# A decode kernel's result: kept as columns and stored from 128 partitions, instead of folded into 16 rows

## The chip, the cores and the metric

The kernel runs on one core of a Trainium2 chip. A core has five engines with queues of their own: TensorE (PE, matmuls; its weight loads are shown as PEld), VectorE (DVE), ScalarE (ACT), GpSimd (POOL) and SyncE (SP, which here only issues transfers). All of them work on SBUF, a memory of 128 partitions; matmuls write to PSUM. Sixteen DMA engines carry the transfers between SBUF and the device's memory (HBM). The metric is device microseconds of one execution. Before the change the median of three runs is 192.62 us (192.46 to 193.06).

## The reference

One token of 512 values goes through attention over a sliding window and through a small MLP that gates it:

```
xn = layernorm(x)                                  # x: [1, 1, 512]
q  = xn @ wq                                       # 32 heads of 128
p  = softmax(q . k[last 4096 positions] * 128**-0.5)
s  = concat_heads(p . v) @ wo                      # [512]
x1 = xn + shifted(gelu(layernorm(xn) @ w1)) @ w2   # all shifts fill with 0 for one token
g  = silu(x1 + gelu(layernorm(x1) @ w3) @ w4)      # [512]
out = x + s * g                                    # [1, 1, 512], bf16
```

With one token every shifted part is zero, so that `x1` is `xn`. The keys and values of 32 heads and 4,096 positions are 33.5 MB each in bf16, and nearly all of the 79 MB that the kernel reads.

## The kernel before

The work goes over the heads in eight groups of four. For each group SyncE issues one load of K (4 MB, three buffers) and, two steps later, one of V (two buffers); the loads stand in program order in SyncE's queue, each behind the wait for its buffer. The scores of a group are computed on two paths: VectorE multiplies a part of the keys with the query and sums (`k_vector`, L334 to L340), and for the rest PE transposes the keys (L356), ScalarE copies them (L359) and PE multiplies (L367). A softmax (`sm_*`) and the product with V (`v_wide`, L440) follow one and two steps later. The order on PE, VectorE and ScalarE is written out by hand in a loop over the steps (L575 to L694); what stands before that loop is ordered by a scheduler.

The front (L101 to L321) loads `x` as 16 rows of 32 values (`x_in`, L80). A matmul and a masked sum bring it to `x_f` (L180), a tile of 128 partitions by 4, where partition p holds the four neighbouring values 4p to 4p+3. From that come the normalised `xn_f` (L183), the query, and the gate. The gate's last products lie in `hr`, a row of 512, and are turned into columns by matmuls (L284). For the gate a second layout is used: column j of `h2_ps` and `g_col` holds the values 128j + p. So `x` is brought into this layout once more (`r_slot`, `r_row`, `r_in`, `xt_ps`, `xn_col`, L239 to L250).

The output product `s` is made in two parts. Heads 0 to 27 are multiplied with `wo` row by row (`y_wide`), summed in `y_sum` (one tile of 512 columns) and transposed into columns (`y_turn`, L553). The last four heads come with the last pieces of V: these are multiplied as columns (`v_part`, L474, into `oP`), `v_turn` (L452) transposes the part that was made wide before, `v_out` (L480) adds both (`both`) and scales them (`o`), and `y_head` (L547) multiplies each head's column with 128 columns of `wo_rows` at a time: 16 matmuls with one moving column, into `y_cols`.

Columns with values 128j + p would be stored as single values. So the kernel multiplies the columns by `g_own` (the gate, spread over four slots with zeros elsewhere) and folds them with a matmul by 0/1 columns (`fold_f`, `fold_bf`) into 16 rows of 32 neighbouring values, `z_rows` (`z_add`, L565). This is done for the first part in fp32 inside the loop (L561, L689), and for the last four heads after it (L696 to L698). VectorE then adds `x_in` (L700), and 16 rows of 64 bytes are stored (L701). `y_cols` and `z_rows` are parts of one PSUM tile, cleared at the start by a matmul with zeros (L305).

Of the kernel before, what the change touches and what calls it, by code (L numbers as in the profile page):

```python
# [8 lines left out]
P = 128  # L9
BF16 = mybir.dt.bfloat16  # L10
FP32 = mybir.dt.float32
# [15 lines left out]
def kernel(  # L27
# [14 lines left out]
    nc = tc.nc  # L42
# [28 lines left out]
    small.tile([P, 240], BF16, name="pad")  # L71
    wts_guard = tc.tile_pool(name="wts", bufs=1)
    wts = wts_guard.__enter__()

# [154 lines left out]
    for j in range(KC):  # L229
        for c in range(KC):  # L230
# [8 lines left out]
    r_slot = wts.tile([XR, KC], BF16, name="r_slot")  # L239
    nc.vector.tensor_reduce(out=r_slot[:], in_=ident_bf[0:XR, 0:XR].rearrange("k (j a) -> k a j", a=KC), axis=AX.X, op=ALU.max)  # L240
    r_row = wts.tile([XR, KC], BF16, name="r_row")
    nc.vector.tensor_reduce(out=r_row[:], in_=ident_bf[0:XR, 0:XR].rearrange("k (j a) -> k j a", a=KC), axis=AX.X, op=ALU.max)
    r_in = wts.tile([XR, KC, XC], BF16, name="r_in")
    nc.vector.tensor_tensor(out=r_in[:], in0=x_in[:].unsqueeze(1).to_broadcast([XR, KC, XC]),
                            in1=r_slot[:].unsqueeze(2).to_broadcast([XR, KC, XC]), op=ALU.mult)
    xt_ps = ps_misc.tile([P, KC], FP32, tag="misc", name="xt_ps")
    nc.tensor.matmul(xt_ps[:], lhsT=r_in[:].rearrange("k a n -> k (a n)"), rhs=r_row[:], start=True, stop=True)
    xn_col = small.tile([P, KC], FP32, name="xn_col")
    nc.vector.tensor_scalar(out=xn_col[:], in0=xt_ps[:], scalar1=negmean[:], scalar2=rstd[:],
                            op0=ALU.add, op1=ALU.mult)  # L250

    a_ps = ps_misc.tile([P, 3, P], FP32, tag="misc", name="a_ps")
    zeros(a_ps[:])
    for c in range(KC):
# [35 lines left out]
    make_masks(16)  # L290
    make_masks(8)
    make_masks(4)
    NQ = P // XC
    g_own = small.tile([P, KC, NQ], FP32, name="g_own")
    nc.gpsimd.tensor_tensor(out=g_own[:], in0=g_col[:].unsqueeze(2).to_broadcast([P, KC, NQ]),
                            in1=masks[4][2][:].unsqueeze(1).to_broadcast([P, KC, NQ]), op=ALU.mult)
    fold_f = const.tile([P, XC], FP32, name="fold_f")
    nc.vector.tensor_reduce(out=fold_f[:], in_=ident_f[:].rearrange("d (i t) -> d t i", t=XC), axis=AX.X, op=ALU.max)
    fold_bf = const.tile([P, XC], BF16, name="fold_bf")
    nc.vector.tensor_copy(out=fold_bf[:], in_=fold_f[:])  # L300
# [127 lines left out]
    def wo_row(h):  # L428
        return wo_rows[:, h - h_part, :]
# [90 lines left out]
                                    op=ALU.add)  # L520
        ox_blk[i] = ox

    small.tile([P, 64], BF16, name="pad_rows")
    y_sum = small.tile([P, D], FP32, name="y_sum")
    small.tile([P, 32], BF16, name="pad_result")

    yr = {}

# [17 lines left out]

    def y_head(h):  # L547
        for j in range(KC):
            nc.tensor.matmul(y_cols[:, j:j + 1], lhsT=wo_row(h)[:, j * P:(j + 1) * P],
                             rhs=o_blk[3][:, h - h_part:h - h_part + 1], start=False, stop=(h == H - 1),  # L550
                             skip_group_check=True)

    def y_turn():  # L553
        yt_ps = ps_misc.tile([P, KC, P], FP32, tag="misc", name="yt_ps")
        for j in range(KC):
            nc.tensor.transpose(yt_ps[:, j, :], y_sum[:, j * P:(j + 1) * P], ident_f[:])
        y_first = small.tile([P, KC], FP32, name="y_first")
        nc.vector.tensor_reduce(out=y_first[:], in_=yt_ps[:].rearrange("p j (i m) -> p j i m", m=32)[:, :, :, 0],
                                axis=AX.X, op=ALU.add)
        t_first = small.tile([P, KC, NQ], FP32, name="t_first")  # L560
        nc.vector.tensor_tensor(out=t_first[:], in0=y_first[:].unsqueeze(2).to_broadcast([P, KC, NQ]), in1=g_own[:],  # L561
                                op=ALU.mult)
        return t_first

    def z_add(t, fold, last):  # L565
        nc.tensor.matmul(z_rows, lhsT=t[:].rearrange("p j q -> p (j q)"), rhs=fold[:], start=False, stop=last,
                         skip_group_check=True)

    NG = H // G
# [5 lines left out]
    for s in range(NG + LAG):  # L575
# [22 lines left out]
        if s < NG:  # L598
            nb = len(batches(s))

            def keys(b0, b1):
                for b in range(b0, b1):
                    k_turn(s, kn, b)
                    if b > 0:
                        k_scores(s, b - 1)

            k_open(s)
            k_vector(s, kn, 0)
            keys(0, 2)
            if s == 7:  # L610
                v_turn(h - 1)
                v_add(h - 1)
                v_out(h - 1)
            elif s > 1:
                sm_den(s - 2)
                sm_rden(s - 2)
            elif s == 1:
                sm_max(0)
            k_vector(s, kn, 1)
            keys(2, 4)  # L620
            if s == 7:
                sm_den(h)
                sm_rden(h)
                keys(4, nb - 2)
                sm_turn(s - 1)
                keys(nb - 2, nb)
            else:
                if s > 0:
                    sm_turn(s - 1)
                keys(4, nb)  # L630
            k_scores(s, nb - 1)
            sm_own(s)
            if s == 7:
                k_vector(s, kn, 2)
                v_wide(h, v)
                sm_exp(s - 1)
                v_turn(h)
                y_open()
                k_vector(s, kn, 3)
                v_add(h)  # L640
                v_out(h)
                ox_spread(1)
                sm_max(s)
                continue
            if s > 0:
# [12 lines left out]
            if s == 6:  # L658
                ox_pick(0)
            if s > 0:  # L660
                sm_max(s)
        elif s == NG:
            ox_pick(1)
            sm_turn(NG - 1)
            sm_exp(NG - 1)
            y_wide(1, False)
            sm_den(NG - 2)
            sm_rden(NG - 2)
            y_wide(0, False)
            warm(3)  # L670
            v_wide(h, v)
            sm_den(NG - 1)
            sm_rden(NG - 1)
            v_turn(h)
            v_add(h)
            v_out(h)
            ox_spread(2)
        else:
            v_open(h)
            warm(2)  # L680
            v_wide(h, v, cuts[1], last=False)
# [4 lines left out]
            t_first = y_turn()  # L686
# [10 lines left out]
    nc.vector.tensor_tensor(out=t_last[:], in0=y_cols.unsqueeze(2).to_broadcast([P, KC, NQ]), in1=g_own[:], op=ALU.mult)  # L697
    z_add(t_last, fold_bf, True)  # L698
    out_sb = small.tile([XR, XC], BF16, name="out_sb")
    nc.vector.tensor_tensor(out=out_sb[:], in0=z_rows, in1=x_in[:], op=ALU.add)  # L700
    load(out.rearrange("a b (r n) -> (a b r) n", r=XR), out_sb[:])  # L701


# [28 lines left out]
```

## Time and profile before

| | |
|---|---|
| profiled execution | 192.31 us |
| its span in the profile | 190.4 us |
| PE busy, clock granted on the mean | 121.9 us (64%), 0.695 |
| VectorE busy | 154.3 us (81%) |
| ScalarE busy | 89.8 us (47%) |
| read from HBM | 78.84 MB, 414 GB/s over the span |
| store of the result, issue to landing | 1.3 us, 1.0 KB |
| first landing of small rows (`x_in`), issue to landing | 2.9 us, 1.0 KB |

The profile is of one execution; 1.91 us of its time lie outside the span. Busy time is time in which an engine runs at least one instruction; neighbouring instructions may overlap. A line of the timeline has start, length, engine, line of the kernel, operation, the tile written and those read, their sizes and a count, and in brackets how long the engine had idled and who ended that. In the chain in order of time each line is a piece that nothing else could have replaced, with its start, its length and what it was. "Issue" in that chain is time without a visible cause.

### The profile page before, as it was taken

The page shows a single profiled execution, that of the slowest core. Times are in us where ns is not written, and L with a number is a line of the kernel's source. Part 1 is how long each engine was busy: PE and PEld are TensorE (multiplying, and loading weights), DVE is VectorE, ACT ScalarE, POOL GpSimd, SP SyncE. Part 2 cuts the span into 40 slices and gives each one's busy share as a digit, 9 for nine tenths or more (in the row PEclk, how much of TensorE's full clock was granted, in tenths as well). Part 3 has the DMA queues.
Part 4 walks back from the last instruction along what each step waited for, and adds up shares of the span by engine and source line. Part 5 has one row for each costly group of instructions (what it writes and reads, how often), then busy time and mean ns, then how long its engine had stood idle before and what let it go on. Part 6 is the DMA issues. An engine that isn't in the chain of part 4 may idle for free.

```text
span 190.4 us, 2822 instructions
## 1 busy us (share of the span) xinstructions
PE 121.9 (64%) x1143; PEld 78.4 (41%) x1143; DVE 154.3 (81%) x184; ACT 89.8 (47%) x192; POOL 2.4 (1%) x11
## 2 busy tenths in 40 slices
PE   2445973977656268436955674572888379748983
PEld 1321442755545243334434333440764068523332
DVE  4830159999999999999999999999999998991111
ACT  2000781778695076517382746452485146754120
POOL 2110000000000000000000000000000000000000
PEclk9999696555555556955596579558555755885999
DMA  6999999999999999999999999999999999999991
GB/s 214 458 404 420 435 427 435 434 441 440 437 442 434 440 434 430 427 434 399 430 427 440 434 437 416 465 434 437 406 434 435 434 420 406 444 434 416 418 389 59
DMA packets 4621, 79.02 MB, mean 415 GB/s; under 512 B 544, under 2 KB 1152, under 8 KB 1664
## 3 DMA queue, kind: packets, MB, share of 16 engines
q1 hardware_dynamic: 4432, 74.65, 91.9%
q10 hardware_dynamic: 176, 4.20, 5.1%
q8 instruction: 9, 0.15, 0.3%
q14 instruction: 4, 0.03, 0.0%
HBM read 78.84 MB, written 0.00 MB: 414 GB/s over the span
## 4 chain that ended last, share of the span: by engine, by line
DVE 56%; DMA 32%; PE 7%; ACT 1%; issue 1%; SPq 1%; DVEq 0%; ACTq 0%
DVE S L340 34%; DMA kv<-in_A_k_cache_dram 24%; DVE prod L338 19%; DMA kv<-in_A_v_cache_dram 8%; PE pt L356 3%; PE ov L444 1%; ACT kt L359 1%; SPq L76 1%; PE sT L367 1%; PE ot_ps L461 1%; DVE m L383 1%; DVE S L381 1%; DVE mx L391 1%; PE oP L477 1%; DVE md L393 0%
## 5 line engine op out<-in xcount | busy, mean ns | idle before, releaser
L340 DVE TENSOR_REDUCE S<-prod 128x20 f32<-128x2560 bf16 (+2 forms) x32 | 87.6, 2736 | 1.1
L359 ACT COPY kt<-pt 128x1024 bf16<-128x1024 bf16 (+1 forms) x51 | 50.0, 1004 | 43.8 <-PE pt L356 42.2
L356 PE MATMUL pt<-ident_f,kv 128*128 128x128 f32 x202 | 48.0, 392 | 11.7 <-DMA kv<-in_A_k_cache_dram 11.7
L338 DVE TENSOR_TENSOR prod<-kv,q_bc 128x2560 bf16<-128x2560 bf16 (+2 forms) x32 | 46.1, 1442 | 2.4 <-DMA kv<-in_A_k_cache_dram 2.1
L356 PEld LDWEIGHTS pt<-ident_f,kv 128*128 128x128 f32 x202 | 35.2, 205 | 15.1 <-DMA kv<-in_A_k_cache_dram 12.3
L367 PE MATMUL sT<-q_pair,kt 128*128 128x8 bf16 x404 | 19.2, 171 | 14.1 <-ACT kt L359 13.9
L367 PEld LDWEIGHTS <-kt 128*128 128x128 bf16 x404 | 16.6, 106 | 25.0 <-ACT kt L359 23.8
L444 PE MATMUL ov<-kv,pT 128*16 128x512 bf16 x248 | 22.7, 528 | 0.7 <-DMA kv<-in_A_v_cache_dram 0.7
L389 PE MATMUL mt_ps<-ident_f,m 128*1 128x128 f32 x8 | 3.0, 372 | 18.3 <-DVE rden L416 17.0
L405 ACT ACTIVATE pT<-S,mb 128x128 bf16<-128x128 f32 x32 | 14.0, 574 | 0.2
L450 ACT COPY ov_sb<-ov 128x512 f32<-128x512 f32 x8 | 4.7, 586 | 18.4 <-PE ov L444 18.4
L444 PEld LDWEIGHTS <-pT 128*16 128x16 bf16 x248 | 6.8, 111 | 13.3 <-issue 11.5
L376 ACT ACTIVATE own<-sT,par 128x48 f32<-128x48 f32 (+2 forms) x32 | 7.5, 352 | 3.7 <-PE sT L367 3.7
L461 PE MATMUL ot_ps<-ident_f,ov_sb 128*128 128x128 f32 x32 | 7.5, 377 | 1.9 <-ACT mb L401 1.6
L208 ACT CAST q_row<-qr_ps 128x512 bf16<-128x512 f32 x1 | 0.6, 586 | 16.8 <-PE qr_ps L206 16.8
L389 PEld LDWEIGHTS mt_ps<-ident_f,m 128*1 128x1 f32 x8 | 0.6, 80 | 18.8 <-DVE rden L416 17.4
L405 ACT ACTIVATION_READ_ACCUMULATOR pT<-S,mb 128x1 f32 x32 | 8.3, 259 | 0.0
L209 DVE CAST q_row<-qr_ps 128x512 bf16<-128x512 f32 x1 | 0.7, 690 | 8.7 <-PE qr_ps L206 8.7
L398 PE MATMUL mb_ps<-md,par_t 5*128 5x4 f32 x16 | 4.3, 335 | 5.0 <-DVE md L393 4.9
L416 DVE RECIPROCAL rden<-den_ps 128x4 f32<-128x4 f32 x8 | 1.4, 175 | 7.2 <-PE den_ps L411 7.2
L398 PEld LDWEIGHTS mb_ps<-md,par_t 5*128 5x128 f32 x16 | 3.8, 291 | 6.0 <-PE sT L367 4.7
L461 PEld LDWEIGHTS ot_ps<-ident_f,ov_sb 128*128 128x128 f32 x32 | 4.8, 188 | 2.5 <-ACT mb L401 2.0
(143 smaller groups left out, 89.8 us busy)
## 6 DMA issues: line engine op xcount, KB each, us to landing
kv<-in_A_k_cache_dram SPq DMA_DIRECT2D x7, 4096.0 KB, 32.2
kv<-in_A_v_cache_dram SPq DMA_DIRECT2D x7, 4096.0 KB, 30.3
wq_sb<-in_A_wq_dram ACTq DMA_DIRECT2D x1, 4096.0 KB, 17.6
kv<-in_A_k_cache_dram SPq DMA_DIRECT2D x2, 2048.0 KB, 25.8
wo<-in_A_wo_dram SPq DMA_DIRECT2D x1, 2048.0 KB, 29.3
kv<-in_A_v_cache_dram SPq DMA_DIRECT2D x1, 2048.0 KB, 13.7
w_sb<-in_B_w_dram SPq DMA_DIRECT2D x1, 1376.0 KB, 12.6
w_sb<-in_B_w_dram SPq DMA_DIRECT2D x1, 1280.0 KB, 18.9
```

Of the source, the lines that this page charges most:

```text
L338: nc.vector.tensor_tensor(out=prod[:, 0:m, :], in0=kn[:, rows, :], in1=q_bc[:, g:g + 1, :].to_broadcast([P, m, Dh]), op=ALU.mult)
L340: nc.vector.tensor_reduce(out=st[g]["S"][:, rows], in_=prod[:, 0:m, :], axis=AX.X, op=ALU.add)
L356: nc.tensor.transpose(pt[:, i, :], kn[:, c:c + 2, :].rearrange("p c d -> p (c d)").bitcast(FP32), ident_f[:])
L359: nc.scalar.copy(out=kts[b][:, 0:n, :], in_=pt[:, 0:n, :].bitcast(BF16))
L367: nc.tensor.matmul(st[g]["sT"][:, c:c + 2, :].rearrange("p c a -> p (c a)"), lhsT=kt[:, i, l::2], rhs=q_pair[:, g, l, :], start=(l == 0), ...
L376: nc.scalar.mul(s["own"][:, 0:m, a], s["sT"][:, 0:m, a], par[:, a:a + 1])
L389: nc.tensor.transpose(mt_ps[:], s["m1"][:], ident_f[:])
L398: nc.tensor.matmul(mb_ps[:], lhsT=par_t[:].rearrange("k b a -> k (b a)"), rhs=md[:], start=True, stop=True)
L405: nc.scalar.activation(out=s["pT"][:, :, a], in_=s["S"][:], func=ACT.Exp, scale=scale, bias=mb[:, a:a + 1], accum_out=s["sum"][:, a:a + 1])
L444: nc.tensor.matmul(ov[r:r + 4 * G], lhsT=s["pT"][:, c:c + 4, :].rearrange("p i a -> p (i a)"), rhs=v[:, c:c + 4, :], start=(i < 4), stop=( ...
L450: nc.scalar.copy(out=s["ov_sb"][:], in_=ov[:])
L461: nc.tensor.transpose(ot_ps[:, step * j:step * j + P], s["ov_sb"][:, j, :], ident_f[:])
```

## The change

The second layout is given up. All that belongs to the output is kept in the layout of `x_f`: partition p, column j holds the value 4p + j. To that end the three products that turn rows into columns take every fourth column of the row (`j::KC`) and not 128 neighbouring ones: `hr` for the gate, `y_sum` in `y_turn`, and `wo_row(h)` in `y_head`. With that `xn_f` itself serves for the gate, and `r_slot`, `r_row`, `r_in`, `xt_ps` and `xn_col` go. `g_own`, `fold_f`, `fold_bf`, `t_first`, `t_last` and both fold matmuls go too. The first part of the product opens the sum in `y_cols` by a matmul with the identity (`y_begin`), which stands after the last pieces of V. After the loop four VectorE operations, one for each column, compute column times gate plus `x`, and the result is stored from 128 partitions with 4 values (8 bytes) each. Three padding tiles grow (`pad`, `pad_rows` and `pad_result`).

```diff
-    r_slot = ... r_row = ... r_in = ...
-    xt_ps = ps_misc.tile([P, KC], FP32, tag="misc", name="xt_ps")
-    nc.tensor.matmul(xt_ps[:], lhsT=r_in[:].rearrange("k a n -> k (a n)"), rhs=r_row[:], start=True, stop=True)
-    xn_col = small.tile([P, KC], FP32, name="xn_col")
-    nc.vector.tensor_scalar(out=xn_col[:], in0=xt_ps[:], scalar1=negmean[:], scalar2=rstd[:],
-                            op0=ALU.add, op1=ALU.mult)
...
-    nc.tensor.matmul(h2_ps[:], lhsT=ident_f[:], rhs=xn_col[:], start=True, stop=False, skip_group_check=True)
+    nc.tensor.matmul(h2_ps[:], lhsT=ident_f[:], rhs=xn_f[:], start=True, stop=False, skip_group_check=True)
     for j in range(KC):
-        nc.tensor.matmul(h2_ps[:, j:j + 1], lhsT=hr[:, j * P:(j + 1) * P], rhs=ind[:], start=False, stop=True,
+        nc.tensor.matmul(h2_ps[:, j:j + 1], lhsT=hr[:, j::KC], rhs=ind[:], start=False, stop=True,
                          skip_group_check=True)
...
-    g_own = ... fold_f = ... fold_bf = ...
-    yz_ps = ps_y.tile([P, KC + XC], FP32, name="yz_ps")
-    nc.tensor.matmul(yz_ps[:], lhsT=zero_bf[:], rhs=zero_bf[:, 0:KC + XC], start=True, stop=False,
-                     skip_group_check=True)
-    y_cols, z_rows = yz_ps[:, 0:KC], yz_ps[0:XR, KC:KC + XC]
+    y_cols = ps_y.tile([P, KC], FP32, name="y_cols")
...
     def y_head(h):
         for j in range(KC):
-            nc.tensor.matmul(y_cols[:, j:j + 1], lhsT=wo_row(h)[:, j * P:(j + 1) * P],
+            nc.tensor.matmul(y_cols[:, j:j + 1], lhsT=wo_row(h)[:, j::KC],
...
     def y_turn():
...
-            nc.tensor.transpose(yt_ps[:, j, :], y_sum[:, j * P:(j + 1) * P], ident_f[:])
+            nc.tensor.transpose(yt_ps[:, j, :], y_sum[:, j::KC], ident_f[:])
...
-        nc.vector.tensor_tensor(out=t_first[:], in0=y_first[:].unsqueeze(2).to_broadcast([P, KC, NQ]), in1=g_own[:],
-                                op=ALU.mult)
-        return t_first
-
-    def z_add(t, fold, last):
-        nc.tensor.matmul(z_rows, lhsT=t[:].rearrange("p j q -> p (j q)"), rhs=fold[:], start=False, stop=last,
+        return y_first
+
+    def y_begin(y_first):
+        nc.tensor.matmul(y_cols[:], lhsT=ident_f[:], rhs=y_first[:], start=True, stop=False,
                          skip_group_check=True)
...
-            z_add(t_first, fold_f, False)
             v_add(h)
             v_part(h, v, cuts[3], CP)
+            y_begin(y_first)
             v_out(h)
...
-    t_last = small.tile([P, KC, NQ], BF16, name="t_last")
-    nc.vector.tensor_tensor(out=t_last[:], in0=y_cols.unsqueeze(2).to_broadcast([P, KC, NQ]), in1=g_own[:], op=ALU.mult)
-    z_add(t_last, fold_bf, True)
-    out_sb = small.tile([XR, XC], BF16, name="out_sb")
-    nc.vector.tensor_tensor(out=out_sb[:], in0=z_rows, in1=x_in[:], op=ALU.add)
-    load(out.rearrange("a b (r n) -> (a b r) n", r=XR), out_sb[:])
+    out_sb = small.tile([P, KC], BF16, name="out_sb")
+    for j in range(KC):
+        nc.vector.scalar_tensor_tensor(out=out_sb[:, j:j + 1], in0=y_cols[:, j:j + 1], scalar=g_col[:, j:j + 1],
+                                       in1=x_f[:, j:j + 1], op0=ALU.mult, op1=ALU.add)
+    load(out.rearrange("a b (p j) -> p (a b j)", p=P), out_sb[:])
```

The scheduler orders the front anew: all 20 matmuls of L259 stand ahead of the 32 of L206 (four stood behind them), and ScalarE takes the Gelu of L262 ahead of the copy of L208, with one load of an activation table fewer. SyncE's transfers and their waits stand in the same order as before.

More of the change, by code (lines that the diff above doesn't have):

```diff
@@ L70 @@
     sm_pool = ctx.enter_context(tc.tile_pool(name="sm", bufs=3))
-    small.tile([P, 240], BF16, name="pad")
+    small.tile([P, 336], BF16, name="pad")
     wts_guard = tc.tile_pool(name="wts", bufs=1)
@@ L237 @@
     nc.vector.tensor_scalar(out=z3_bf[:], in0=xc3[:], scalar1=rstd3[:], scalar2=None, op0=ALU.mult)
[L239 to L245, printed above, removed]
-    xt_ps = ps_misc.tile([P, KC], FP32, tag="misc", name="xt_ps")
-    nc.tensor.matmul(xt_ps[:], lhsT=r_in[:].rearrange("k a n -> k (a n)"), rhs=r_row[:], start=True, stop=True)
-    xn_col = small.tile([P, KC], FP32, name="xn_col")
-    nc.vector.tensor_scalar(out=xn_col[:], in0=xt_ps[:], scalar1=negmean[:], scalar2=rstd[:],
-                            op0=ALU.add, op1=ALU.mult)
     a_ps = ps_misc.tile([P, 3, P], FP32, tag="misc", name="a_ps")
@@ L292 @@
     make_masks(4)
[L293 to L300, printed above, removed]
-    yz_ps = ps_y.tile([P, KC + XC], FP32, name="yz_ps")
-    nc.tensor.matmul(yz_ps[:], lhsT=zero_bf[:], rhs=zero_bf[:, 0:KC + XC], start=True, stop=False,
-                     skip_group_check=True)
-    y_cols, z_rows = yz_ps[:, 0:KC], yz_ps[0:XR, KC:KC + XC]
+    y_cols = ps_y.tile([P, KC], FP32, name="y_cols")
     par = const.tile([P, G], FP32, name="par")
@@ L521, in ox_pick @@
         ox_blk[i] = ox
-    small.tile([P, 64], BF16, name="pad_rows")
+    small.tile([P, 112], BF16, name="pad_rows")
     y_sum = small.tile([P, D], FP32, name="y_sum")
-    small.tile([P, 32], BF16, name="pad_result")
+    small.tile([P, 96], BF16, name="pad_result")
     yr = {}
@@ L559, in y_turn @@
                                 axis=AX.X, op=ALU.add)
-        t_first = small.tile([P, KC, NQ], FP32, name="t_first")
-        nc.vector.tensor_tensor(out=t_first[:], in0=y_first[:].unsqueeze(2).to_broadcast([P, KC, NQ]), in1=g_own[:],
-                                op=ALU.mult)
-        return t_first
-    def z_add(t, fold, last):
-        nc.tensor.matmul(z_rows, lhsT=t[:].rearrange("p j q -> p (j q)"), rhs=fold[:], start=False, stop=last,
+        return y_first
+    def y_begin(y_first):
+        nc.tensor.matmul(y_cols[:], lhsT=ident_f[:], rhs=y_first[:], start=True, stop=False,
                          skip_group_check=True)
@@ L685 @@
             v_wide(h, v, cuts[2], cuts[1])
-            t_first = y_turn()
+            y_first = y_turn()
             v_part(h, v, cuts[2], cuts[3])
             v_turn(h)
-            z_add(t_first, fold_f, False)
             v_add(h)
             v_part(h, v, cuts[3], CP)
+            y_begin(y_first)
             v_out(h)
```

## The prediction

> **What bounds the kernel now.** I read the page's header and the 40 slices first, to see which engine or queue has no room; then the chain of work that ended last; then the chain in order of time and the timeline of the last microseconds; then the DMA issues.
>
> ```profile
> span 190.4 us, 2822 instructions
> PE 121.9 (64%) x1143; PEld 78.4 (41%) x1143; DVE 154.3 (81%) x184; ACT 89.8 (47%) x192; POOL 2.4 (1%) x11
> ...
> DMA  6999999999999999999999999999999999999991
> ...
> DVE 56%; DMA 32%; PE 7%; ACT 1%; issue 1%; SPq 1%; DVEq 0%; ACTq 0%
> ```
>
> Although VectorE (DVE) has 56% of the chain, the DMA row is at 9 in every slice but the first and the last: the loads never pause, so VectorE and the loads keep pace with each other, and an engine that gets ahead in the middle finds no earlier data. What is left to gain or lose lies before the stream starts and after it ends. The end in order of time:
>
> ```profile
> 184.77 0.56 PE oP L477 x16
> 185.32 0.49 PE ot_ps L461 x4
> 185.82 0.16 PE yz_ps L566 x2
> 185.98 0.01 issue
> 185.99 0.57 PE oP L477 x16
> 186.56 0.02 issue
> 186.58 0.17 DVE both L489
> 186.75 0.02 issue
> 186.78 0.17 DVE o L492
> 186.95 0.04 issue
> 186.99 0.60 PE yz_ps L549 x16
> 187.60 0.02 issue
> 187.62 0.19 DVE t_last L697
> 187.81 0.04 issue
> 187.85 0.20 PE yz_ps L566
> 188.05 0.02 issue
> 188.07 0.18 DVE out_sb L700
> ```
>
> The groups at 184.77 and 185.99 begin 0.04 us after a piece of V lands (184.72 and 185.94 in the record of landings), and the 16 matmuls of L549 begin when both `o` and the first piece of `wo_rows` are there (landed 186.95); the second piece lands at 187.29. So up to 187.3 the stream paces the end, with compute a few hundredths behind, and from 187.6 a serial tail runs alone: VectorE, PE, VectorE, the store.
>
> ```profile
> 7.20 0.66 PE L231 MATMUL hs_ps<-shifted_bf,w_sb 128*128 128x1 bf16 x16 [0.25 <-DVE ln_vtot_x L162]
> ...
> 7.25 0.14 DVE L164 TENSOR_SCALAR ln_rstd_x<-ln_vtot_x 128x1 f32<-128x1 f32 x1
> 7.32 0.28 DVE L129 TENSOR_REDUCE blk<-ident_bf 128x32 bf16<-128x128 bf16 x1
> ...
> 8.07 0.23 DVE L184 TENSOR_SCALAR xn_f<-ln_xc_x,ln_rstd_x 128x4 f32<-128x4 f32 x1 [0.29 <-POOL ln_rstd_x L166]
> 8.21 0.19 DVE L132 COPY to<-blk 128x128 bf16<-128x128 bf16 x1
> ...
> 186.99 0.59 PE L549 MATMUL yz_ps<-o,wo_rows 128*128 128x1 bf16 x16 [0.45 <-DVE o L492]
> ...
> 188.28 0.35 SPq L76 DMA_DIRECT2D out_dram<-out_sb  x1
> ```
>
> These rows of the timeline price the new forms: a weight read that skips by four (L231) beside a dense one (L549), a small VectorE operation with a per-partition scalar (L184) beside one with a constant (L164), each with the start of its follower, and the store.
>
> **The front (0 to 32 us): nothing.** Gone are `r_slot`, `r_row`, `r_in`, `xn_col`, `fold_f`, `fold_bf` on VectorE, two matmuls (L305, L247) and `g_own` on POOL. All of it ran between 1 and 13 us, or at 28.84 for `g_own`, while the first VectorE operation on K waits until 25.72 for its data, landed at 25.63. `q_bc` was ready at 24.15, 1.5 us of cover. In the built order all 20 matmuls of L259 now stand before the 32 of L206, where 4 stood behind: the last 4 took 0.88 us, PE idled 2.12 us before L206 for `wq`, so they fit. ScalarE now takes the Gelu (L262) first and needs one table load fewer (1.28 us), so `q_bc` comes no later. The four `hr` products now read with a step of four fp32 (8 loads, 1.03 us); their reader is `g_col`, needed on ScalarE before 32.78, and it ended at 28.76: 4 us of cover. SyncE's loads and their waits stand in the same order; an earlier first V load (28.63) only queues behind K pieces still in flight. Front and middle: 0.
>
> **y_turn: nothing, with 0.5 us of cover.** The four transposes now read `y_sum` with a step of 16 bytes. They start at 184.07, 109 ns apart, so PE could take the next group at about 184.56, but that waits for V until 184.76: 0.20 us. The L566 pair (0.16 us by the chain) leaves the space before the next landing; from the last transpose of L461 (185.65) to 185.98 PE then has another 0.3 us. Only when the four together need over 0.5 us more is the end moved. `y_begin` (an fp32 matmul, two passes; the like L148 took 0.56 us at 4.51, and 0.43 at 9.55) stands behind the last oP group and runs while VectorE makes `both` and `o` (186.58 to 186.94), beside PE idle of 0.45 us: 0, at worst 0.1, since the y_head matmuls queue behind it. The vanished `t_first` was off the path.
>
> **y_head: +0.07 us.** Sixteen weight loads read every fourth bf16 column. L231 is this very form: 16 in 0.66 us against 0.59 for L549. The last four wait for the second piece of `wo_rows`, at 187.33 now; at L231's 33 ns the first twelve take until 187.39, so that wait is overtaken. Ends: 0 and +0.13 (16 times 8 ns).
> [...] The trace has 33 against 25 ns, and I take the trace. [...]
>
> **The four column operations: 0.00 us.** Removed: 187.62 to 188.25, that is 0.63 us (`t_last`, the fold matmul, `out_sb` and two hand-overs). Added: four operations in a row without waits. L184 with a scalar from SBUF took 0.23 and its follower started 0.14 later, L164 with a constant 0.14 and 0.07. With the former, 3 x 0.13 + 0.24 = 0.63. Low end: 3 x 0.065 + 0.165 = 0.36, that is -0.27. High end: xn_col, with PSUM and two such scalars, took 0.28; four end to end with 0.02 between make 1.18, that is +0.55. I take 0 because L184 is nearest: one scalar, few elements.
>
> **The store: +0.25 us.** 16 rows of 64 bytes become 128 rows of 8. Now: issue at 188.28 (0.35 us), packets from 189.12 to 189.27, landed 189.61. Loads with 128 rows issued in 0.38 to 0.43, and the very first of them, on empty queues, moved its first packet 1.01 us after its issue began, against 0.84 here: +0.17. Each of 16 DMA engines moves 8 packets for 1; 64-byte ones took 8 ns here and 11 at the start: 7 x 11 ns, +0.08. After the last packet 0.33 us passed to the landing, as for `wo_rows` (186.95 to 187.29), so I add nothing there. Low end 0: the bytes are the same and the packets more, so a gain is excluded. High end +1.6: the other transfer of 16 small rows, `x_in`, landed after 2.9 us instead of 1.3, behind other traffic. I stay near the low end, since nothing else moves at 189 us.
>
> **Sum.** 0.07 + 0.00 + 0.25 = +0.32. On the profiled execution's 192.31 us (span 190.4 and 1.91 around it) that is 192.63; this execution was 0.31 under the median of 192.62, so the forecast is 192.94, 0.17% slower, below the 0.3% (0.58 us) that a measurement of this kernel can tell from no change.
>
> **Rivals.**
> Store by small writes (slower). Place: 189.1 to 189.6. If 8-byte writes hinder each other, each of 128 costing some 5 to 10 ns in turn at the memory, it is 0.6 to 1.3 us more: about 193.8. It decides from +0.26 beyond my price. For it: no row shows an 8-byte write. Against: after 64-byte writes the landing is no later than after loads.
> [...]
>
> Columns end to end (slower). Four operations at xn_col's 0.28: +0.55, in all 0.07 + 0.55 + 0.25 = +0.87, 193.5. For it: PSUM source and a scalar. Against: followers start before an operation ends all over the start.
>
> y_turn over its cover (slower). With the 392 ns mean of K's transposes apart instead of 109, the four need 1.57 against 0.44, 1.13 more and 0.63 over the cover: 193.6. Against: K's mean is latency; they overlap.
>
> Columns at the pitch of constants (not slower): -0.27 + 0.07 + 0.25, 192.7; with the store at 0, 192.4.
>
> Front earlier (faster). If V's first load was late, its release one table load (1.28 us) earlier would move the stream by that: 192.94 - 1.28 = 191.7. Against: the DMA row has no gap there.
>
> **How the numbers follow.** Forecast 0.42, store 0.28, columns end to end 0.10, y_turn 0.05, columns overlapped 0.08, front 0.07. Faster is the front, 0.07; slower the store, the end-to-end columns and y_turn, 0.43; same 0.50. The range of 192.4 to 193.8 leaves out the front and about half of a tenth of the store's upper part. The forecast's own range is 192.6 to 193.2.
>
> **What would show it.** L549's successor: 16 in about 0.66 us. Four operations on `out_sb` within 0.63 us of y_head's end, starts about 0.13 apart. The store's landing 1.5 to 1.6 us after its issue instead of 1.3. First VectorE work on K still near 25.7 us and both V landings still just ahead of the oP groups. The forecast is wrong if the store needs over 1.8 us, if the columns take over 0.9 us, or if K's first product moves.

## The result, and the profile after

The changed kernel takes 194.22 us (median of six runs, 194.02 to 195.92) against 192.59 before (192.43 to 193.06, six runs). The ratio, made from the means of the runs, is 1.0101, with a 95% interval of 1.0074 to 1.0127: slower by 1%. The forecast was 192.94, its range 192.4 to 193.8, and 0.50 of the chance lay on "no difference". The profiled execution took 194.26 us, with a span of 192.3.

The page's header, the clock and DMA slices and the chain by engine, of the changed kernel:

```profile
span 192.3 us, 2807 instructions
PE 120.1 (62%) x1140; PEld 77.7 (40%) x1140; DVE 153.5 (80%) x179; ACT 88.4 (46%) x191; POOL 2.2 (1%) x10
...
PEclk9999695555555558955695598555555859966997
DMA  6999999999999999999999999999999998999970
...
DVE 55%; DMA 30%; PE 9%; ACT 2%; issue 1%; SPq 1%; ACTq 0%; DVEq 0%
```

No engine got busier. What is new is the last two digits of the DMA row: 7 and 0 where 9 and 1 stood. The last slice, 4.8 us long, now holds no DMA work to speak of, though the span ends in it. The chain in order of time, from the last piece of V on:

```profile
186.31 0.57 PE oP L449 x16
186.88 0.02 issue
186.90 0.17 DVE both L461
187.08 0.02 issue
187.10 0.17 DVE o L464
187.27 0.04 issue
187.31 0.68 PE y_cols L521 x16
187.99 0.03 issue
188.02 0.22 DVE out_sb L667
188.24 0.13 DVEq L695
188.37 0.25 DVE out_sb L667 x2
```

The three removed steps of the tail (VectorE, PE, VectorE) are now one group on VectorE. The timeline has its whole length and the store's issue, and further up the two steps that were moved or changed ahead of it:

```profile
184.36 0.75 PE L528 MATMUL yt_ps<-ident_f,y_sum 128*128 128x128 f32 x4
...
186.72 0.36 PE L535 MATMUL y_cols<-y_first,ident_f 128*128 128x4 f32 x2
...
187.31 0.66 PE L521 MATMUL y_cols<-o,wo_rows 128*128 128x1 bf16 x16 [0.23 <-DVE o L464]
188.02 0.60 DVE L667 SCALAR_TENSOR_TENSOR out_sb<-y_cols,g_col,x_f 128x1 bf16<-128x1 f32 x4 [0.76 <-PE y_cols L521]
188.65 0.35 SPq L76 DMA_DIRECT2D out_dram<-out_sb  x1
```

Four column operations in 0.60 us and the store's issue at once behind them. The windows from there on (busy time of PE, PEld, VectorE, ScalarE and GpSimd, granted clock, DMA share, GB/s) show what the end consists of:

```profile
189.45:189.75 0.30, 0.00 (x0) 0.00 (x0) 0.00 (x0) 0.00 (x0) 0.00 (x0) 1.00 0.26 4
189.75:191.55 1.80, 0.00 (x0) 0.00 (x0) 0.00 (x0) 0.00 (x0) 0.00 (x0) 0.58 0.00 0
```

The store's packets pass in 0.2 us, and then for 1.8 us nothing runs on any engine and no DMA engine moves a packet: the kernel waits until the last of the store's 16 landings, which came from 189.90 to 191.50 us (before: from 189.44 to 189.61). The DMA issues give the same from issue to landing, 2.9 us where the kernel before has 1.3:

```profile
out_dram<-out_sb SPq DMA_DIRECT2D x1, 1.0 KB, 2.9
```

The kernel before, for comparison, from its windows and its DMA issues:

```profile
189.10:189.30 0.20, 0.00 (x0) 0.00 (x0) 0.00 (x0) 0.00 (x0) 0.00 (x0) 1.00 0.08 5
189.30:189.65 0.35, 0.00 (x0) 0.00 (x0) 0.00 (x0) 0.00 (x0) 0.00 (x0) 1.00 0.00 0
...
out_dram<-out_sb SPq DMA_DIRECT2D x1, 1.0 KB, 1.3
```

Put together from the chain, the timeline and the record of landings, in us of the two profiled executions:

| piece | before | after | difference | forecast |
|---|---|---|---|---|
| start of `y_head` | 186.99 | 187.31 | +0.32 | 0 |
| `y_head`, to the start of the next operation | 0.63 | 0.71 | +0.08 | +0.07 |
| from there to the store's issue | 0.66 | 0.63 | -0.03 | 0 |
| store, issue to last landing | 1.33 | 2.85 | +1.52 | +0.25 |
| last landing to the end of the span | 0.83 | 0.83 | 0 | 0 |

That sums to +1.89, the difference of the two spans. So by the profile one term of the forecast was missed, and it is the store. But the first row, too, was to be 0. It came with the loads: the last piece of V landed at 186.26 instead of 185.94 us, the first of `wo_rows` at 187.24 instead of 186.94. One pair of executions cannot tell whether that is chance.

### The profile page after: what moved, and what is told of

It reads as the page before. It is cut to its first block, busy times and chain, and to the rows that moved or that the text cites. A ratio compares the mean times of both kernels' runs of the same rounds, so it can differ in the third digit from the quotient of the medians.

```text
span 192.3 us, 2807 instructions
## 1 busy us (share of the span) xinstructions
PE 120.1 (62%) x1140; PEld 77.7 (40%) x1140; DVE 153.5 (80%) x179; ACT 88.4 (46%) x191; POOL 2.2 (1%) x10
## 4 chain that ended last, share of the span: by engine, by line
DVE 55%; DMA 30%; PE 9%; ACT 2%; issue 1%; SPq 1%; ACTq 0%; DVEq 0%
DVE S L312 33%; DVE prod L310 18%; DMA kv<-in_A_k_cache_dram 12%; DMA kv<-in_A_v_cache_dram 9%; DMA wq_sb<-in_A_wq_dram 9%; PE pt L328 2%; ACT kt L331 2%; PE qr_ps L206 2%; PE ov L416 1%; PE sT L339 1%; SPq L76 1%; DVE m L355 1%; DVE S L353 1%; PE qt_ps L219 1%; PE hr_ps L264 1%
## 5 line engine op out<-in xcount | busy, mean ns | idle before, releaser
L328 PE MATMUL pt<-ident_f,kv 128*128 128x128 f32 x202 | 46.2, 381 | 11.9 <-DMA kv<-in_A_k_cache_dram 11.9
L328 PEld LDWEIGHTS pt<-ident_f,kv 128*128 128x128 f32 x202 | 33.8, 198 | 15.1 <-DMA kv<-in_A_k_cache_dram 12.8
L249 ACT ACTIVATE a_row<-a_ps 128x384 bf16<-128x384 f32 x1 | 0.5, 490 | 13.8 <-remote 13.8
```

Of the source, the lines that this page charges most:

```text
L328: nc.tensor.transpose(pt[:, i, :], kn[:, c:c + 2, :].rearrange("p c d -> p (c d)").bitcast(FP32), ident_f[:])
```

## The experiments

Two theories stood against each other at first. A: the store alone is the cause; its small writes land late. B: what precedes it (columns, transposes, the new front) has its part. Runs named e1, e3, e4, e10, e11, e16, e17 and e18 fill a wider tile for the store, so that most of the values they store are not the result; their time is read for the order and the store alone. The same holds for e2 and e5, which add `x_f` to the first columns of the fold's PSUM tile, and for the runs that store to a buffer of their own.

**The store alone, twice over.** e2 gives the kernel before the store of the changed one, and e1 gives the changed kernel the store of the one before.

```diff
  e2, against the kernel before
-    out_sb = small.tile([XR, XC], BF16, name="out_sb")
-    nc.vector.tensor_tensor(out=out_sb[:], in0=z_rows, in1=x_in[:], op=ALU.add)
-    load(out.rearrange("a b (r n) -> (a b r) n", r=XR), out_sb[:])
+    out_sb = small.tile([P, KC], BF16, name="out_sb")
+    nc.vector.tensor_tensor(out=out_sb[:], in0=yz_ps[:, KC:2 * KC], in1=x_f[:], op=ALU.add)
+    load(out.rearrange("a b (p j) -> p (a b j)", p=P), out_sb[:])
  e1, against the changed kernel
+    out_sb = small.tile([P, 32], BF16, name="out_sb")      # early, cleared
-    load(out.rearrange("a b (p j) -> p (a b j)", p=P), out_sb[:])
+    load(out.rearrange("a b (r n) -> (a b r) n", r=16), out_sb[0:16, 0:32])
```

> The kernel before with one thing of the change: its last VectorE operation writes 128 partitions by 4 (from the first columns of the fold's PSUM tile, so the output is not the result), and the store takes 128 rows of 8 bytes. Theory A, small writes: store landing 2.85 us after its issue, time 192.6 + 1.5 = 194.1 us. Theory C, columns and weight reads: landing as before and 192.6 to 192.8 us. Theory B, the stream: store +1.2 at most, the last landing of wo_rows unchanged, 193.8 us.

> The changed kernel with one thing undone: the four column operations stand, but the store takes 16 rows of 64 bytes from the tile that they wrote to (of the 16 first partitions, the rest of the row zeros; so the output is not the result). Theory A, small writes: the 1.53 us that the store gained (1.33 to 2.85 us from issue to landing) goes back; the store lands 1.3 us after its issue, and the time is 194.22 - 1.53 = 192.7 us, within 0.2 us of before. Theory B, the stream: the last pieces of wo_rows landed 0.3 us later in the changed kernel's profile; if its front or its middle made that, 0.3 us stay and the time is 192.9 to 193.1 us. Theory C, the columns and weight reads: if these cost what the profile does not show, 193.5 us or more.

e2: 195.34 us (195.13 to 195.64), ratio 1.0142 (1.0121 to 1.0164), more than the whole change. Its store landed after 3.1 us, but its first operation on K also came later (26.10 for 25.72) and its last `wo_rows` landing as well (188.45 for 187.28): something else was in it. The new `out_sb` is smaller in memory, and every tile allocated behind it, two of the K and V buffers and `wo_rows` among them, had moved by 32 bytes. e5 puts the tiles back with 16 more columns of `pad`, and e12 does the opposite: the kernel before as it is, with `pad` 16 columns smaller.

```diff
  e5, against e2
-    small.tile([P, 240], BF16, name="pad")
+    small.tile([P, 256], BF16, name="pad")
  e12, against the kernel before
-    small.tile([P, 240], BF16, name="pad")
+    small.tile([P, 224], BF16, name="pad")
```

> The second experiment again, with a padding tile 32 bytes larger, so that the tiles behind it keep the addresses that they have in the kernel before. Theory A, small writes: landing 1.5 us later than before, 192.47 + 1.5 = 194.0 us in executions whose stream ends where it ends before. If the 195.3 us of the second experiment came with the moved addresses, they go here; if they came with the granted clock between 160 and 180 us, some executions here reach 195 us too, with a low clock there.

> The kernel before with its first padding tile 32 bytes smaller and nothing else, so that the tiles behind it start 32 bytes lower, as in the second experiment. If the 1.3 us by which the second experiment was slower than the fifth came from the addresses: 192.6 + 1.3 = 193.9 us, first product on K near 26.1 us, last landing of wo_rows near 188.4 us. If not: 192.6 us.

e5: 194.03 us (193.80 to 194.22) against 192.60, ratio 1.0071 (1.0057 to 1.0085); the store landed after 3.0 us. So the store costs 1.4 us in a kernel in which nothing else of the program differs but the size of `pad` and the operation ahead of the store, which adds `x_f` to columns (0.16 us instead of 0.18). Its windows show the same empty end:

```profile
189.20:189.50 0.30, 0.00 (x0) 0.00 (x0) 0.00 (x0) 0.00 (x0) 0.00 (x0) 1.00 0.26 4
189.50:191.50 2.00, 0.00 (x0) 0.00 (x0) 0.00 (x0) 0.00 (x0) 0.00 (x0) 0.79 0.00 0
```

e12, with not one instruction changed, took 193.47 us (193.05 to 193.86), ratio 1.0049 (1.0033 to 1.0064): the moved addresses alone cost 0.9 us. The chain of e12 ends in the load of `wo_rows`, where that of the kernel before runs through `o`:

```profile
170.65 17.45 DMA wo_rows<-in_A_wo_dram
188.11 0.05 issue
188.15 0.59 PE yz_ps L549 x16
```

Its expectation asked for 1.3 us, the whole excess of e2 over e5; 0.9 of it came, and the rest, 0.2% of the time, lies within the intervals of the three ratios. In the changed kernel, and in every other run here, the paddings keep all buffers of the stream at the addresses of before, so this effect is no part of the result.

e1: 193.03 us, ratio 1.0039 (1.0011 to 1.0066); the store landed after 1.3 us. Theory A asked for a ratio near 1. Six of its twelve runs lie between 192.44 and 192.68, as before, and six between 193.37 and 195.25. e11 repeats it with the same code:

> The first experiment once more, as the control for the one with the front put back. Theories D and E: fastest executions 192.4 to 192.6 us, half of them up to 3 us above, median 192.6 to 193.1 us.

193.01 us (192.25 to 193.80), ratio 1.0026 (1.0012 to 1.0041). So A falls as the whole story: without the store's cost 0.3 to 0.4% remains.

**Which property of the store.** The following kernels change only the store of the changed kernel, and each was timed once. e3, e4 and e18 store to the output in 32 and 64 rows; the others to a buffer of their own in HBM (`scratch`), while `x` goes to the output early.

```diff
-    load(out.rearrange("a b (p j) -> p (a b j)", p=P), out_sb[:])
+    load(out.rearrange("a b (r n) -> (a b r) n", r=32), out_sb[0:32, 0:16])              # e3
+    load(out.rearrange("a b (r n) -> (a b r) n", r=64), out_sb[0:64, 0:8])               # e4
+    load(scratch[:, 0:32], out_sb[:, 0:32])           # e6, scratch of 128 x 32 values
+    load(scratch[:, 0:4], out_sb[:, 0:4])             # e7, of 128 x 32
+    load(scratch[:, 0:4], out_sb[:, 0:4])             # e8, of 128 x 4
+    load(scratch[:, 0:4], out_sb[:, 0:4])             # e9, of 128 x 8
+    load(scratch[0:128, 0:8], out_sb[0:128, 0:8])     # e13, of 128 x 8
+    load(scratch[0:64, 0:4], out_sb[0:64, 0:4])       # e14, of 128 x 4
+    load(scratch[0:128, 0:4], out_sb[0:128, 0:4])     # e15, of 128 x 16
+    load(out.rearrange("a b (k r n) -> (a b r) k n", k=4, n=8), out_sb[0:64, 0:8])       # e18
```

> The changed kernel with a store of 32 rows of 32 bytes (output not the result). If every write counts (12 ns each: 1.52 us for 112 more), landing 1.33 + 16 x 0.0136 = 1.55 us after issue. If what counts is that several writes fall into one 64-byte line, two per line: nearer to a half of the whole, 2.0 us or more. If only rows under 32 bytes are slow: 1.33 us.

> The changed kernel with a store of 64 rows of 16 bytes (output not the result). If every write counts: 1.33 + 48 x 0.0136 = 1.98 us from issue to landing. If sharing a 64-byte line counts, 2.5 us or more, near the 2.85 of 128 rows.

> The changed kernel, its 128-row store replaced by 128 rows of 64 bytes, each a whole line, into a scratch tensor of 8 KB (the result is not stored; the output gets x early on). If the number of writes counts: 1.8 us from the last packet to the last landing, 2.85 us from issue. If what counts is that a write is smaller than 16 bytes or shares its line: 0.34 us and about 1.4 us.

> The same with 128 rows of 8 bytes, each at the start of a 64-byte line of its own in the scratch tensor. If 8-byte writes are slow as such: 1.8 us from last packet to last landing. If they hinder each other because eight fall into one 64-byte line: 0.34 us.

> The control for the two before: 128 rows of 8 bytes side by side in a scratch tensor of 1 KB. Every theory: as in the changed kernel, landings spread over 1.6 us, 2.85 us from issue.

> As the run with lines of their own, but the 128 rows of 8 bytes start 16 bytes apart in the scratch tensor: four share a 64-byte line, none shares a unit of 16 bytes (the result is not stored). If the 8-byte writes hinder each other by sharing a 64-byte line: 1 us or more from the last packet to the last landing. If it takes two writes in one unit of 16 bytes (64 rows of 16 bytes side by side had landed 0.34 us after their last packet): 0.4 to 0.5 us.

> The changed kernel whose store writes 128 rows of 16 bytes, packed (four to a 64-byte line), into a 2 KB scratch buffer; what is written there is not the result. 64 rows of 16 bytes, packed, landed 1.72 us after an issue of 0.55; 128 rows of 8 bytes at a 16-byte step landed after 2.35. If it is the size of a row that counts (16 bytes is written straight, 8 bytes is not), the landing is at 1.4 to 1.6 us. If it is that several rows share a 64-byte line, and their number, it is at 2.0 to 2.5 us.

> The changed kernel whose store writes 64 rows of 8 bytes, packed, into a 512-byte scratch buffer; what is written there is not the result. 128 such rows landed 2.85 to 3.06 us after the issue, 16 rows of 64 bytes 1.33. If each 8-byte write costs its share in turn, half the rows cost half of the excess: 2.1 us. If it is decided by the eight rows of one line, which wait for one another while lines go side by side, it stays at 2.6 to 3.0 us.

> The changed kernel whose store writes 128 rows of 8 bytes at a step of 32 bytes, two to a 64-byte line, into scratch; what is written there is not the result. Eight to a line landed after 2.85 to 3.06 us, four to a line after 2.35, one to a line after 1.46. If writes to one line wait for one another, two to a line land at 1.6 to 1.9 us; if any sharing of a line costs the same, at 2.3 or later; if a line alone was fast for another reason than sharing, also at 2.3 or later.

> The changed kernel with the store of 64 packed rows of 16 bytes, but neighbouring partitions write places 256 bytes apart: partition 4r+k writes row 16k+r, so that the four rows of a 64-byte line come from partitions 4 apart; the output's order is thereby mixed and most of the values in it are not the result. With neighbouring partitions in one line this store landed 1.72 us after an issue of 0.55, 0.34 after its last packet. If that was on time because the rows of a line followed each other on one DMA engine, and writes of different engines to one line wait, the last landing now comes 0.8 us or more after the last packet, as with four rows to a line in the stores of 128 rows (1.3). If four rows of 16 bytes in a line never wait in a store of 64 rows, it stays at 0.34.

The measure is the time from the end of the last packet to the last landing, from the record of packets and landings; it leaves out the issue, which is 0.33 to 0.35 us with 16, 32 and 128 rows and 0.51 to 0.63 with 64. It repeats well: all seven profiled stores of 16 rows have 0.32. "In a line" counts the rows in 64 bytes of memory; 64 is the widest step that was run, so that the runs do not show whether the memory itself has a boundary there. The times of these executions, 192.97 to 195.96 us, also hold what is told of the front below, and are not read here.

| store | rows x bytes | in a line | last packet to last landing, us | issue to landing, us |
|---|---|---|---|---|
| before, to the output | 16 x 64 | 1 | 0.32 | 1.33 |
| e6 | 128 x 64 | 1 | 0.36 | 1.41 |
| e7 | 128 x 8 | 1 | 0.44 | 1.46 |
| e15 | 128 x 8 | 2 | 1.04 | 2.08 |
| e9 | 128 x 8 | 4 | 1.33 | 2.36 |
| e13 | 128 x 16 | 4 | 1.32 | 2.35 |
| changed, to the output | 128 x 8 | 8 | 1.81 | 2.85 |
| e5 and e2, to the output | 128 x 8 | 8 | 1.99 and 2.05 | 3.03 and 3.09 |
| e8 | 128 x 8 | 8 | 2.04 | 3.06 |
| e14 | 64 x 8 | 8 | 2.23 | 3.57 |
| e3, to the output | 32 x 32 | 2 | 0.34 | 1.35 |
| e4, to the output | 64 x 16 | 4 | 0.34 | 1.72 |
| e18, to the output | 64 x 16 | 4 | 0.35 | 1.81 |

e7 and e8, and e15 between them, decide the main point. From the DMA issues of the three, in that order:

```profile
scratch<-out_sb SPq DMA_DIRECT2D x1, 1.0 KB, 1.5
```

```profile
scratch<-out_sb SPq DMA_DIRECT2D x1, 1.0 KB, 3.1
```

```profile
scratch<-out_sb SPq DMA_DIRECT2D x1, 1.0 KB, 2.1
```

The same 128 rows of 8 bytes, from the same partitions through the same queue, land 1.6 us earlier when each has a line of its own. Neither the size of a row nor the number of rows is the cause: 8 bytes are fast in e7 (0.44 us after the last packet), and 64 rows are no faster than 128 (e14, 2.23 us, where half of the excess was asked for by the theory of a price per write). e9 was meant to test whether 16 bytes to a row are enough; they are not, and e13, with rows that fill these 16 bytes, lands like e9 to 0.01 us. With the stores of 128 rows the delay grows with the rows that share a line: 1, 2, 4 and 8 of them give 0.4, 1.0, 1.3 and 1.8 to 2.0 us. And it comes in steps: of e9's 16 landings eight came within 0.27 us of the last packet, four at about 0.8, four at 1.2 to 1.3. From these three groups it is an estimate that writes to one line take turns of about half a microsecond; the trace does not show the memory, and no run shows the turns themselves. What stays open is the exemption of e3, e4 and e18: two or four rows in a line, at 32 and 64 rows, land on time. e18 spread the four rows of each line over partitions 4 apart and changed nothing, so that it is not their neighbourhood in SBUF; whether it is the number of rows, their size, or the buffer was not separated. Three expectations were missed: e4's 1.72 us from issue to landing fits neither of its two values, e15's 2.08 lies between its two, and e14's 3.57 is above its range.

**The front.** e10 keeps the store of e1 and restores the front of the kernel before (the block from `r_slot` to `xn_col`, the dense reads of `hr`, `g_own`, `fold_f`, `fold_bf` and the opening matmul); the strided `y_head` and `y_turn`, `y_begin` and the four column operations stay. e16 and e17 restore one part of that each.

```diff
  e16, against e1
+    r_slot = ...  r_row = ...  r_in = ...  xt_ps = ...  xn_col = ...
-    nc.tensor.matmul(h2_ps[:], lhsT=ident_f[:], rhs=xn_f[:], start=True, stop=False, skip_group_check=True)
+    nc.tensor.matmul(h2_ps[:], lhsT=ident_f[:], rhs=xn_col[:], start=True, stop=False, skip_group_check=True)
  e17, against e1
+    g_own = ...  fold_f = ...  fold_bf = ...
+    nc.tensor.matmul(y_cols[:], lhsT=zero_bf[:], rhs=zero_bf[:, 0:KC], start=True, stop=True)
  e10, against e1: both, and
-        nc.tensor.matmul(h2_ps[:, j:j + 1], lhsT=hr[:, j::KC], rhs=ind[:], start=False, stop=True,
+        nc.tensor.matmul(h2_ps[:, j:j + 1], lhsT=hr[:, j * P:(j + 1) * P], rhs=ind[:], start=False, stop=True,
```

> The first experiment (changed kernel, store of 16 rows of 64 bytes; output not the result), with the front of the kernel before put back: its order on PE and ScalarE, the dense reads of hr, and r_slot to fold_bf, of which the end uses nothing. Theory D: the new front shifts the stretches of low granted clock so that more executions have one between 160 and 180 us, where PE then ends late; this kernel's executions stay within 1 us of the fastest, as those of before do, median 192.5 to 192.7 us. Theory E: the front has no part in it; half of the executions are 1 us or more above the fastest, as in the first experiment, median 193.0 us.

> The changed kernel with the store of 16 rows of 64 bytes, and of the front of the kernel before only the block from r_slot to xn_col restored, and its product in h2_ps; the strided reads of hr stay, g_own and the folds stay away. With this block ScalarE's order is again that of the kernel before. If it is the order of the front's work that puts stretches of low granted clock at the end: as the kernel before, 192.5 to 192.65 us, ratio 1.000 within 0.001. If it is the strided reads or the absent folds, as the store of 16 rows alone: 192.9 to 193.1, ratio 1.003 to 1.004.

> The changed kernel with the store of 16 rows of 64 bytes, and of the front of the kernel before only g_own, fold_f, fold_bf and the opening matmul of the result's tile restored; the order of ScalarE and of the gates stays that of the changed kernel, and so do the strided reads of hr. If it is the order from the block r_slot to xn_col: 192.9 to 193.1 us, ratio 1.003 to 1.004. If it is the absent folds: as the kernel before, ratio 1.000 within 0.001.

| | us, median | ratio to before, 95% |
|---|---|---|
| e1 and e11, changed front | 193.03 and 193.01 | 1.0039 (1.0011 to 1.0066) and 1.0026 (1.0012 to 1.0041) |
| e10, whole front of before | 192.56 | 1.0000 (0.9991 to 1.0009) |
| e16, the block `r_slot` to `xn_col` alone | 192.66 | 1.0009 (0.9999 to 1.0018) |
| e17, folds and opening matmul alone | 192.88 | 1.0040 (1.0020 to 1.0059) |

Two things follow. First, e10 has the whole new end of the kernel but for its store, and costs nothing: `y_head`, the columns, the transposes and `y_begin` together are 0 within 0.17 us. Second, the changed front does cost 0.3 to 0.4%, and it is the block that was removed. e16 adds work, four VectorE operations and a matmul, and is faster for it. So it is argued that what counts is the order that the block brings back around it, ScalarE's with the copy of L208 ahead of the Gelu of L262 among it; no run restores that order without the block. The strided `hr` reads (still in e16) and the missing folds (restored in e17) are not it.

How 0.3% come from an order at 25 us is seen only in part. With the changed front's order, `y_head` begins at 187.8 us or later in 5 of 14 profiled executions (187.83 to 188.86, in e3, e4, e8, e9 and e18); with the order of before it began between 186.99 and 187.24 in all four that have the same addresses (before, e5, e10, e16). In the late ones the loads are on time: in e4 the last piece of `wo_rows` landed at 187.32. PE is late. (e8 and e9 are weaker evidence: like e13 and e14 they have a second delay, their first operation on K starts at 27.24 and 27.52 us and in the 14 others of these 18 at 25.70 to 25.96; no run shows why.) Windows of 5 us of the changed kernel's own profile, which is one of the punctual executions (PE, PEld, VectorE, ScalarE, GpSimd, granted clock, DMA share, GB/s):

```profile
160.00:165.00 5.00, 3.54 (x59) 2.56 (x61) 4.37 (x6) 4.01 (x6) 0.00 (x0) 1.00 0.97 405
165.00:170.00 5.00, 2.95 (x39) 1.37 (x31) 4.86 (x6) 3.35 (x14) 0.00 (x0) 0.96 1.06 455
170.00:175.00 5.00, 3.55 (x26) 1.66 (x30) 1.82 (x8) 1.92 (x9) 0.00 (x0) 0.50 0.97 419
175.00:180.00 5.00, 4.62 (x55) 1.85 (x44) 0.18 (x1) 0.58 (x1) 0.00 (x0) 0.86 0.95 401
```

and of e4:

```profile
160.00:165.00 5.00, 4.67 (x48) 3.66 (x46) 3.68 (x6) 3.24 (x4) 0.00 (x0) 0.50 0.94 391
165.00:170.00 5.00, 4.24 (x42) 1.68 (x42) 4.93 (x3) 1.99 (x6) 0.00 (x0) 0.50 1.08 463
170.00:175.00 5.00, 2.96 (x19) 1.35 (x19) 2.20 (x10) 2.93 (x14) 0.00 (x0) 0.84 0.97 419
175.00:180.00 5.00, 5.00 (x41) 1.59 (x41) 0.18 (x1) 1.10 (x6) 0.00 (x0) 0.50 0.93 393
```

In e4 the granted clock is 0.50 from 160 to 170 us, where the other has 1.00 and 0.96, and it is 0.50 again from 175 on, when PE is busy for 5.00 of 5.00 us. The chain of e4, in order of time, runs over PE from there on, and past the points where the last V pieces land:

```profile
166.14 3.55 PE ov L418 x26
...
175.58 1.81 PE yr_ps L517 x15
177.39 1.39 PE wm L506 x3
178.78 2.66 PE ov L418 x27
...
185.22 0.59 ACT y_sum L655
185.82 0.04 issue
185.86 0.75 PE yt_ps L530 x4
186.61 0.38 PE oP L451 x16
186.99 0.50 PE ot_ps L435 x4
187.49 0.39 PE oP L451 x16
```

Here the transposes of `y_turn`, hidden in the changed kernel's own profile, stand on the path with their 0.75 us. The other late executions have the low clock too. Over the stretch from 155 to 180 us the mean granted clock is 0.57 in e4, e8, e9 and e18 and 0.53 in e3; in the 13 executions that are not late it is 0.59 to 0.78, and the next latest of them, e14 and e11 with 187.66 and 187.64, have 0.61 and 0.59. So the shown part is: the late executions are those with the lowest clock over that stretch. The clock does not give the size, since e3 has the lowest and is the least late, and e16, with 0.59, was on time. That the order of the front decides how often this happens is shown by the times alone (e1, e11 and e17 against e10 and e16); four profiles with the order of before are too few. That it does so by moving the low stretches, and why it would, is not shown.

None of the runs is faster than the kernel before; e10 equals it.

## Why the prediction was wrong

*The store, +0.25: the step that failed.* It measured +1.52 in the profile and 1.4 us in e5. Of its three pieces, the first packet came 0.84 us after the issue, as before, so the added 0.17 was not there; the packets took 0.20 us for 0.16, half of the 0.08 that was added; and "I add nothing there", said of the time from the last packet to the landing, is where all of it lies: 1.81 instead of 0.32. The bounds of the term held it, with a high end of +1.6, but the range, which ended at 193.8, left out that end. What was wrong is the choice between the ends: "I stay near the low end, since nothing else moves at 189 us" supposed that a landing is late only behind other traffic, while this store is late with no other packet in flight. The landing of 64-byte rows was no evidence for rows that share 64 bytes.

The size of a row does not separate the stores of 128 rows: 64 bytes (e6) and 8 bytes on lines of their own (e7) landed 0.36 and 0.44 us after the last packet. What separates them is whether rows share a line; those that do came 1.04 to 2.05 us after (e15 and e2 at the ends). What such rows wait for no run shows.

*Store by small writes, the rival:* right in place, and on the right side, at 0.28. Its price of 0.6 to 1.3 us, on top of the forecast's 0.25, covers the 1.4; its time, 193.8, is short of the 194.22. Its cause, 128 writes each paying in turn, does not hold: e7 has 128 such writes and landed 0.44 us after the last packet, and e14 has half of them and landed 2.23 after. The 5 to 10 ns a write were the author's estimate; no run shows such a price.

*The front, nothing: wrong.* Every step of its working stands: the first operation on K came at 25.94 and waited for data landed at 25.84 (the profile names ScalarE's copy of `hr`, which ended just before, but in e1, with the same front, the operation starts at 25.80 and that copy runs until 26.26); `q_bc` was ready at 24.06; one table load went. But "front and middle: 0" supposed that what has cover at 25 us has no later effect. e1, e11 and e17 have 0.26 to 0.40%, 0.5 to 0.8 us, which e10 and e16 do not have. No view of a single execution of the kernel before could have shown it; a bound of some tenths of a per cent on any new order of the front would have been honest. Together, 0.71% (e5) and 0.26 to 0.40% make 0.97 to 1.11%, and the change has 1.01%.

*`y_head`, +0.07: right.* +0.08. The 16 matmuls with the step of 8 bytes start 33 ns apart (L521), the dense ones of before 25 ns (L549), so that the low end of 0 falls.

*The columns, 0: right.* -0.03. Starts are 0.125 to 0.137 us apart, as the 0.13 taken from L184, and each operation takes 0.21 to 0.22. The rival "end to end" (+0.55) and "pitch of constants" (-0.27) both fall.

*`y_turn` with 0.5 us of cover: right where PE is on time.* The four transposes took 0.75 us instead of 0.66, not the 1.57 of the rival, and `y_begin` ran while VectorE made `both`. The caution that they lie on the path when the cover is gone is what e4 shows; there it is 0.1 us.

*Front earlier, the faster rival:* the first K product and the stream did not move forward; it falls.

## What to carry to other kernels

A result that leaves last should be written so that few rows share 64 bytes of memory, best in rows that fill them (in stores of 128 rows, 0.36 us after the last packet in e6, against 0.44 with 8 of every 64 bytes in e7): 128 rows of 8 bytes packed side by side landed 1.5 us later than 16 rows of 64, and as nothing ran behind the store, 1.4 us of that were time (e5). When a cost lies between two bounds and no row of the trace has the same form, the low end needs a reason of its own. And when a change lets a scheduler order the front anew, or moves a streamed buffer by 32 bytes, one has to expect some tenths of a per cent (here 0.26 to 0.40 for the front and 0.49 for the addresses) that belong to neither the removed nor the added work, and to check with the old order and the old addresses before the edit is blamed.

## What the runs showed of the hardware

- In stores of 128 rows, rows that share 64 bytes of memory land late: 0.44 us after the last packet with one row of 8 bytes to 64 (e7), 1.04 with two (e15), 1.33 with four (e9), 1.81 to 2.05 with eight (the changed kernel, e5, e8, e2). Stores of 32 rows of 32 bytes (e3) and of 64 rows of 16 bytes (e4, e18), two and four to 64, landed at 0.34 to 0.35; one of 64 rows of 8 bytes, eight to 64 (e14), at 2.23.
- In the two profiles with tiles moved by 32 bytes the stream is slower: from 50 to 170 us e12 and e2 have 428 to 429 GB/s where the kernel before, e5, e10 and e16 have 432 (single windows of 30 us go both ways, as from 110 to 140 us with 435 in e12 and 426 before). In e12 the last piece of `wo_rows` landed at 188.43 instead of 187.28, and the kernel's time is 0.49% longer.
- The granted clock stood at 0.50 in e4 from 175 to 180 us, with PE busy for 5.00 of 5.00 us, and also in the changed kernel from 170 to 175 us, with PE busy for 3.55. Which stretches get it differs between executions of the same code: from 155 to 180 us the mean is 0.78 in e1 and 0.59 in e11.
